# When the fifth and sixth unit make their sums: later quarter sums and sums of x, keys turned ahead of sums, one weight difference on VectorE

## The chip, the cores and the metric

The kernel runs on one core of one Trainium2 chip. The metric is the device time of one execution in microseconds; lower is better. The core's engines have queues of their own that run in order: TensorE (PE in the profile; its weight loads are PEld), VectorE (DVE), ScalarE (ACT), GpSimd (POOL) and SyncE (SP), which here mostly issues DMAs. They wait for each other on semaphores.

## The reference

Two layers, one after the other, all in float32. The first is a recurrence over 768 tokens for 4 batches and 8 heads of 48 dimensions. The second takes the 3072 x 384 result `x` through two weight matrices of 384 x 2048 and 2048 x 384.

```python
# first layer, for each batch and head; w is a decay per key dimension, u a bonus
for t in range(S):
    cur = einsum('d,e->de', u * k[t], v[t])
    y[t] = einsum('d,de->e', r[t], state + cur)
    state = w[t][:, None] * state + einsum('d,e->de', k[t], v[t])
# second layer
h = x @ w_in
g = h * (1.0 / (1.0 + np.exp(-h)))
out = g @ w_out
```

## The kernel before, in words

**Units.** The 768 tokens are cut into 6 blocks of 128, and the 4 batches into 2 pairs: 12 units, `i` = 0 to 11, each of one block for one pair. The text calls them unit 0 to unit 11, so the fifth and sixth unit are units 4 and 5.

**First layer.** Within a block the recurrence is done by levels: level `l` pairs neighbouring runs of 2^l tokens. Per unit, raw `w`, `k` and `r` are turned into `tw`, `tk`, `tr` (`turn`, line 361, transposes on VectorE); products of decays are made on GpSimd (`product`, 410); keys and queries are multiplied by them (`grow_keys`, 642, and `grow_own`, 651, on GpSimd; `grow_queries`, 624, and `prepare`, 779, on VectorE); TensorE multiplies queries and keys (`burst`, line 700); VectorE or ScalarE keep the right parts in the tile `score` (`keep_level`, 718 and 800). Products within groups of 8 tokens go another way: GpSimd multiplies (`block_bonus`, 493), VectorE sums (`block_sum` 0 to 4, line 530, into `block_sums`), DMAs move the sums through DRAM into `block_both` (`block_move`), and `block_turn` (563) and `block_write` (569) put the two halves of the heads into `score`. At the unit's end TensorE makes the output (`y_state` and `y_values`, 843 to 864) and the state's update (`update`, 909), and VectorE adds the update (932) after the old state was multiplied by the decays (914 on GpSimd up to unit 3, 927 on ScalarE later).

**Second layer.** For units 0 to 2 the first product is made plainly (`up`, line 1078, eight pieces, each followed by a Silu on ScalarE into a tile `gt`). From unit 3 on it is made by a fast scheme with 20 products (`first_part`, line 1185) of sums of weights and sums of x. The sums of weights are made once, by `in_weight_sum` (line 1124): `q7`, `q8` and so on, each a difference or sum of two 128x512 parts. The sums of x are made for each unit by `sums_of_x`, steps 0 to 7 (lines 1146 to 1166, VectorE). Between the 20 products VectorE joins partial results (`join`, line 1212) and ScalarE copies them (1206, 1209, 1228), in PSUM banks that the next products add to. The second product is made by seven quarter products (`quarter`, line 1329), three of which take sums of `gt` that `sums` makes on VectorE (line 1300): s1 is an addition; s2 = s1 - lower[0]; s3 is a difference; s4 = upper[0] - s2. In the list `made` of `sums` the places are 0: s1, 1: s3, 2: s2, 3: s4. The quarter products run in the order gt, gt, s2, s1, s3, s4, gt; results leave by ScalarE (1334) or by an addition on VectorE (1337, to `temps` or `ob`), and a later quarter product adds to the same bank, so it waits for that read. `sums(i, m)` makes the sums of piece m: two pieces of 128x512 from unit 3 on, four of 128x256 (m = 0 to 3) for units 1 and 2.

**Order.** No scheduler decides: each engine's queue is the order in which the Python code issues. For each `i` from 3 to 11 the loop at the end takes the seven quarter products of unit i-2 and the first products of unit i-1 as a list of steps, and the groups of unit i's first layer from `mix(i)`; each group has a count, and after the group's operations so many steps are issued:

```python
        for group, count in groups:
            do(*group)
            for step in steps[:count]:
                do(*step)
            steps = steps[count:]
```

So unit 4's stretch holds the second product of unit 2, the first product of unit 3 and the first layer of unit 4. Within it, VectorE's queue holds sums of gt, joins, sums of x and first-layer work, in the order of the groups. `NPAIR` is 4, `NFAST` 3, `FH` 8, and `j` is i-1. `in_weight_sum` operations are added to the groups of units 3 and 4 by place, with the engine beside the place.

Of the kernel before, what the change touches and what calls it, by code (L numbers as in the profile page):

```python
# [38 lines left out]
def kernel(  # L39
# [11 lines left out]
    nc = tc.nc  # L51
# [5 lines left out]
    NB = 2  # L57
# [11 lines left out]
    NPAIR = 4  # L69
# [389 lines left out]
    at = 768  # L459
# [495 lines left out]
    def both(fn, i, *args):  # L955
        return [(fn, i, b, *args) for b in range(NB)]
# [4 lines left out]
    def mix(i):  # L961
# [18 lines left out]
        def products_of(j, *ls):  # L980
            return [(product, j, l) for l in ls]

        end = [[*at(ahead, *bonus_steps(i + 1, 0, 1, 2, 3))],
               [*at(i < len(units) - NB, (turn_apart, i), (turn_k, i)), (y_state, i), *both(y_values, i), *at(ahead, *turns(i + 1)), *at(ahead and i > NFAST, *sum_steps(i + 1, 0, 1)),
                *at(i <= NFAST, (sums, i - 1, FH // 2 - 2)), *both(update, i), *at(not ahead, (move_x, i))]]
        if i < NPAIR:
            groups = [[*both(turn, i, "w"), (product, i, 0)],
                      [*both(turn, i, "k"), (odd_ones, i)], [*both(turn, i, "r"), (start_levels, i), (prepare_keys, i, 1)],
                      [(prepare, i, 1), *[(product, i, l) for l in range(1, NL)]],
                      [(burst, i, 1), (keep_level, i, 1)],  # L990
                      [(keep_level, i, 2), (go_on, i, 2)],
                      [(prepare, i, 3), (reverse_v, i), (bonus, i, 0), (bonus_sum, i, 0)],
                      [(bonus, i, 1), (burst, i, 3), (keep_level, i, 3), (bonus, i, 2)],
                      [(keep_level, i, 4), (go_on, i, 4), (bonus_sum, i, 1), (load_rk, i + 1), (load_u,)],
                      [(prepare, i, 5), (make_block_mask,), (bonus_spread, i)],
                      [(burst, i, 5), (keep_level, i, 5, 0), (keep_level, i, 6, 0), (go_on, i, 6), *at(i == NPAIR - 1, *both(turn, i + 1, "w")), (bonus_write, i, (0,)), (keep_level, i, 5, 1), (keep_level, i, 6, 1), (bonus_write, i, (1,))], *end]
            groups = list(zip(groups, (1, 1, 0, 2, 1, 1, 1, 1, 1, 2, 2, 1, 1)))
        else:
            j = i - 1
            if i <= NPAIR:  # L1000
                groups = [([*both(turn, i, "r"), (grow_own, i, 0), (x_out, j)], 2),
                          ([*start(i), *bonus_steps(i, 4), (x_in, j), (reverse_v, i)], 1),
                          ([(grow_queries, i, 2), (sums_of_x, j, 0)], 1),
                          ([(odd_keys, i, 2), (grow_keys, i, 2, False), (sums_of_x, j, 1)], 1),
                          ([(sums_of_x, j, 2), *sum_steps(i, 2), (prepare, i, 3), *bonus_steps(i, 5, 6, 7), (sums_of_x, j, 3, 4, 5, 6)], 2),
                          ([(burst, i, 3), (keep_level, i, 3)], 2),
                          ([*sum_steps(i, 3)], 1),
                          ([], 1),
                          ([*sum_steps(i, 4), (keep_level, i, 4)], 2),
                          ([(go_on, i, 4)], 1),  # L1010
                          ([], 1),
                          ([*at(ahead, (load_rk, i + 1, (0, 1), nc.scalar)), (block_move, i, False), (block_move, i, True), *at(ahead, (load_rk, i + 1, (2,)))], 1),
                          ([], 1),
                          ([(sums_of_x, j, 7)], 1),
                          ([(prepare, i, 5)], 2),
                          ([], 1),
                          ([(burst, i, 5), (keep_level, i, 5, 0), (keep_level, i, 6, 0), (go_on, i, 6), (block_turn, i), (block_write, i, 1)], 2),
                          ([(keep_level, i, 5, 1), (keep_level, i, 6, 1)], 1),
                          ([(block_write, i, 0), *at(i == NPAIR, *both(turn, i + 1, "w"))], 1),
                          ([*end[0], *at(i == NPAIR, *products_of(i + 1, 0))], 2), (end[1], 0)]  # L1020
            else:
                keys_2 = [(odd_keys, i, 2), (grow_keys, i, 2, False), (grow_queries, i, 2), *sum_steps(i, 2)]
                keys_3 = [(prepare, i, 3), *bonus_steps(i, 5)]

                def loads(name, *gs):
                    return [(load_blocks, i + 1, name, g) for g in gs if ahead]

                groups = [([*both(turn, i, "r"), *at(j == NPAIR, (sums, j - 1, 1, (1, 3))), (grow_own, i, 0), (x_out, j, nc.sync), *loads("w", 0, 1)], 2),
                          ([*at(j >= NPAIR, (add_update, j)), *start(i), *bonus_steps(i, 4), (x_in, j, nc.sync), *loads("w", 2, 3), (reverse_v, i)], 1),
                          ([*keys_2, *loads("k", 0, 1)], 1),  # L1030
                          ([*keys_3, *at(NPAIR + 1 < i < len(units) - 1, (sums_of_x, j, 0, 1)), *loads("k", 2)], 1),
                          ([*at(i in (NPAIR + 1, len(units) - 1), (sums_of_x, j, 0, 1)), (sums_of_x, j, 2), *bonus_steps(i, 6, 7), (sums_of_x, j, 3, 4, 5, 6), *loads("k", 3)], 2),
                          ([(burst, i, 3), *sum_steps(i, 3), (keep_level, i, 3), *sum_steps(i, 4)], 2),
                          ([(block_move, i, False), *at(ahead, (load_rk, i + 1, (0, 1))), *at(ahead and i > NPAIR + 1, (turn, i + 1, 0, "w"))], 1),
                          ([*loads("r", 0)], 1),
                          ([(block_move, i, True), *at(i == NPAIR + 1, (turn, i + 1, 0, "w")), *at(ahead, (turn, i + 1, 1, "w"), *products_of(i + 1, 0, 1, 2)), (keep_level, i, 4)], 2),
                          ([(go_on, i, 4), *at(ahead, *products_of(i + 1, 3, 4, 5, 6))], 1),
                          ([*at(ahead, (load_rk, i + 1, (2,)))], 1),
                          ([*loads("r", 1)], 1),
                          ([*at(ahead, (load_values, i + 1))], 1),  # L1040
                          ([(sums_of_x, j, 7)], 1),
                          ([(prepare, i, 5), *loads("r", 2)], 2),
                          ([*loads("r", 3)], 1),
                          ([(burst, i, 5), (keep_level, i, 5, 0), (keep_level, i, 6, 0), *at(ahead, *bonus_steps(i + 1, 0)), (go_on, i, 6), (block_turn, i), *at(i > NPAIR + 1, (block_write, i, 1))], 2),
                          ([(keep_level, i, 5, 1), (keep_level, i, 6, 1)], 1),
                          ([*at(i == NPAIR + 1, (block_write, i, 1)), (block_write, i, 0)], 1),
                          ([*at(ahead, *bonus_steps(i + 1, 1, 2, 3)), ], 2),
                          (end[1], 0)]

# [254 lines left out]
    def quarter(i, which):  # L1304
# [34 lines left out]
        if which >= 5 or final and which in (1, 4):  # L1339
# [96 lines left out]
    for i in range(3, len(units)):  # L1436
# [51 lines left out]
```

## Time and profile before

| | |
|---|---|
| median of 3 runs | 572.47 us (571.69 to 572.49) |
| the profiled execution | 571.82 us, span 570.0 us |
| granted TensorE clock | 0.997 |
| TensorE busy | 556.4 us, 98% |
| VectorE busy | 477.6 us, 84% |
| GpSimd busy | 396.8 us, 70% |
| ScalarE busy | 270.6 us, 47% |
| moved by DMA | 57.59 MB, 99 GB/s of HBM traffic over the span |

The span runs from the first to the last instruction. A timeline row gives start, length, engine, line, operation, output<-input, the shape, how many instructions were merged into the row, and in brackets the idle time of the engine before it and what ended that. A wait row gives who waited for whom, the total, the number of times and the longest. A windows row gives a stretch, its length, the busy time and instructions of PE, PEld, DVE, ACT and POOL, the granted clock, DMA share and GB/s. Line numbers are those of the kernel before; in the kernel after, lines from 983 to 1346 are one higher, and lines after `SOON` two or more.

### The profile page before, as it was taken

The page shows a single profiled execution, that of the slowest core. Times are in us where ns is not written, and L with a number is a line of the kernel's source. Part 1 is how long each engine was busy: PE and PEld are TensorE (multiplying, and loading weights), DVE is VectorE, ACT ScalarE, POOL GpSimd, SP SyncE. Part 2 cuts the span into 40 slices and gives each one's busy share as a digit, 9 for nine tenths or more (in the row PEclk, how much of TensorE's full clock was granted, in tenths as well). Part 3 has the DMA queues.
Part 4 walks back from the last instruction along what each step waited for, and adds up shares of the span by engine and source line. Part 5 has one row for each costly group of instructions (what it writes and reads, how often), then busy time and mean ns, then how long its engine had stood idle before and what let it go on. Part 6 is the DMA issues. An engine that isn't in the chain of part 4 may idle for free.

```text
span 570.0 us, 18875 instructions
## 1 busy us (share of the span) xinstructions
PE 556.4 (98%) x7782; PEld 517.9 (91%) x7782; DVE 477.6 (84%) x745; ACT 270.6 (47%) x604; POOL 396.8 (70%) x450
## 2 busy tenths in 40 slices
PE   8989999999998999899999999999999999999997
PEld 7768776698888999899999999999999999999997
DVE  7979798898999899879989989989989989882250
ACT  5779695442451373273274274274274272371330
POOL 6998868637999998795696696696696696700000
PEclk9989999999999999999999999999999999999999
DMA  9957776444255365265464465365465462102000
GB/s 224 316 114 204 183 230 113 49 84 101 74 90 100 69 112 94 58 130 93 73 129 89 87 120 94 71 128 94 93 106 96 91 109 65 37 6 56 29 9 21
DMA packets 206485, 57.59 MB, mean 101 GB/s; under 512 B 186048, under 2 KB 198208, under 8 KB 206400
## 3 DMA queue, kind: packets, MB, share of 16 engines
q1 hardware_dynamic: 203712, 54.23, 46.3%
q10 hardware_dynamic: 2688, 2.16, 1.6%
q8 instruction: 61, 1.00, 0.8%
q14 instruction: 24, 0.20, 0.1%
HBM read 47.14 MB, written 9.18 MB: 99 GB/s over the span
## 4 chain that ended last, share of the span: by engine, by line
PE 76%; DVE 9%; POOL 8%; issue 2%; DMA 2%; ACT 1%; SPq 1%; DVEq 0%; POOLq 0%
PE p_o L1329 24%; PE p_o L1185 15%; PE p_h L1185 10%; PE p_h L1078 6%; PE p_h L1329 4%; PE p_m L1267 4%; POOL tk L642 2%; PE p_sc L700 2%; PE p_m L864 2%; DVE temps L1300 2%; PE p_sc L1329 2%; DVE score L718 2%; PE p_m L843 1%; PE p_m L700 1%; DMA raw<-in_r_dram 1%
## 5 line engine op out<-in xcount | busy, mean ns | idle before, releaser
L642 POOL TENSOR_TENSOR tk<-tk,tw 128x256 f32<-128x256 f32 x112 | 93.2, 853 | 7.1 <-DVE tw L410 3.1
L1329 PE MATMUL p_o<-own,temps 128*128 128x192 f32 x496 | 82.9, 326 | 1.5 <-DVE temps L1300 1.5
L1329 PEld LDWEIGHTS p_o<-own,temps 128*128 128x128 f32 x496 | 80.8, 190 | 1.8 <-DVE temps L1300 1.8
L1185 PE MATMUL p_o<-xt,w_in_sb 128*64 128x128 f32 x1152 | 72.1, 273 | 0.6 <-POOL w_in_sb L1124 0.6
L1078 PE MATMUL p_h<-xt,w_in_sb 128*128 128x256 f32 x288 | 67.7, 391 | 0.8 <-POOL w_in_sb L260 0.8
L1185 PEld LDWEIGHTS p_o<-xt,w_in_sb 128*64 128x64 f32 x1152 | 64.7, 137 | 0.8 <-POOL w_in_sb L1124 0.8
L1078 PEld LDWEIGHTS p_h<-xt,w_in_sb 128*128 128x128 f32 x288 | 54.7, 194 | 9.4 <-POOL w_in_sb L260 1.1
L410 POOL TENSOR_TENSOR tw<-tw 128x256 f32<-128x256 f32 (+6 forms) x71 | 38.8, 546 | 33.0 <-DVE tw L361 29.6
L1329 PE MATMUL p_o<-w_out_sb,gt 128*128 128x192 f32 x308 | 54.4, 329 | 1.4 <-DVE ob L1337 1.4
L493 POOL TENSOR_TENSOR ruk<-tokens_rk 128x384 f32<-128x384 f32 x48 | 54.3, 1151 | 0.0
L1329 PEld LDWEIGHTS p_o<-w_out_sb,gt 128*128 128x128 f32 x308 | 50.1, 190 | 2.3 <-DVE ob L1337 1.7
L624 DVE TENSOR_TENSOR tr<-tr,tw 128x512 f32<-128x512 f32 x57 | 51.1, 896 | 0.6
L651 POOL TENSOR_TENSOR tk<-tk,tw 128x256 f32<-128x256 f32 x32 | 24.8, 806 | 30.7 <-DVE tk L361 30.7
L1300 DVE TENSOR_TENSOR temps<-gt 128x512 f32<-128x512 f32 (+1 forms) x48 | 44.6, 965 | 0.0
L1334 ACT COPY partial<-p_o 128x192 f32<-128x192 f32 x31 | 9.9, 319 | 70.5 <-PE p_o L1329 70.5
L612 ACT COPY tk<-tk 128x256 f32<-128x256 f32 x52 | 21.0, 403 | 38.0 <-POOL tk L642 29.0
L1209 ACT ACTIVATE gt<-p_o 128x512 f32<-128x512 f32 x45 | 26.1, 601 | 25.6 <-PE p_o L1185 25.6
L718 DVE COPY_PREDICATED score<-mask,p_sc 128x512 f32<-128x512 int8 x42 | 31.2, 798 | 0.8 <-PE p_sc L700 0.6
L1329 PE MATMUL p_o<-w_out_sb,temps 128*128 128x192 f32 x176 | 30.4, 326 | 0.0
L493 POOL TENSOR_TENSOR spare<-tokens_rk 128x384 f32<-128x384 f32 x24 | 29.1, 1228 | 0.6
L1329 PE MATMUL p_h<-w_out_sb,gt 128*128 128x192 f32 x168 | 29.1, 326 | 0.0
L1329 PEld LDWEIGHTS p_o<-w_out_sb,temps 128*128 128x128 f32 x176 | 28.9, 190 | 0.0
(252 smaller groups left out, 1308.0 us busy)
## 6 DMA issues: line engine op xcount, KB each, us to landing
w_out_sb<-in_moe_w_in_dram SPq DMA_DIRECT2D x6, 768.0 KB, 6.9
turned<-yt SPq DMA_DIRECT2D x18, 192.0 KB, 2.7
xt<-turned SPq DMA_DIRECT2D x9, 384.0 KB, 3.3
w_out_sb<-in_moe_w_out_dram SPq DMA_DIRECT2D x4, 768.0 KB, 5.1
own<-in_moe_w_out_dram SPq DMA_DIRECT2D x4, 768.0 KB, 6.5
tokens_w<-in_w_dram SPq DMA_DIRECT2D x8, 384.0 KB, 4.4
tokens_rk<-in_r_dram SPq DMA_DIRECT2D x7, 384.0 KB, 4.7
tokens_rk<-in_k_dram SPq DMA_DIRECT2D x7, 384.0 KB, 5.7
```

Of the source, the lines that this page charges most:

```text
L410: engine.tensor_tensor(out=up, in0=t[:, :, 0::2], in1=t[:, :, 1::2], op=ALU.mult)
L493: mul = lambda out, one, two: nc.gpsimd.tensor_tensor(out=out, in0=one, in1=two, op=ALU.mult)
L624: nc.vector.tensor_tensor(out=odd, in0=odd, in1=tw[i][l][:, :, 0::2][:, :, :, None].to_broadcast([128, Q, L >> (l + 1), c]), op=ALU.mult)
L642: nc.gpsimd.tensor_tensor(out=out, in0=have, in1=odd_products(i, l, b, *blocks), op=ALU.mult)
L651: nc.gpsimd.tensor_tensor(out=have, in0=have, in1=odd_products(i, l, b, [2, NP * ni]), op=ALU.mult)
L718: nc.vector.copy_predicated(out=dst, mask=masks[l][:, :, None].to_broadcast([128, NB, NP, ni, c]), data=sc[e].rearrange("p (b q) (i c) -> ...
L1078: nc.tensor.matmul(p_h[:, a, :], lhsT=w_in_sb[:, c, f * 128:(f + 1) * 128], rhs=xt[i][:, c, :], start=(a == 0 and c == 0), stop=(a == 1 an ...
L1185: nc.tensor.matmul(p[h:h + PD, q, :], lhsT=left[:, f:f + PD], rhs=right, start=first and q == 0, stop=q == 3, skip_group_check=True)
L1209: nc.scalar.activation(out=g(f, t), in_=have, func=AF.Silu)
L1267: nc.tensor.matmul(po[i, b], lhsT=gt[i, f // 2][:, f % 2, b * L:(b + 1) * L], rhs=w_out_sb[:, f, :], start=(f == 0), stop=(f == FC - 1))
L1300: nc.vector.tensor_tensor(out=out, in0=one, in1=two, op=op)
L1329: nc.tensor.matmul(p, lhsT=left(f), rhs=right[:, f, :], start=which in (0, 1, 3) and f == 0, stop=f == FH - 1, skip_group_check=True)
```

## The change

It moves operations of units 4 and 5 within their queues and gives one to another engine; no operation is added or removed, no DMA is moved, and the queues of TensorE, ScalarE and SyncE keep their order.

- Sums of pieces 2 and 3 of unit 2: s1 and s2 stay at the end of unit 3's stretch; s3 of both pieces goes into unit 4's group 0 behind the turning of r, and s4 of both into group 1.
- Sums of x of unit 3: steps 0 to 2 go together into group 4 of unit 4, steps 3 to 6 from group 4 behind the masked copies of group 5, and step 7 from behind the 10th first product to behind `prepare(4, 5)` and the 13th.
- s1 and s2 of piece 1 of unit 3 go behind the turning of unit 5's keys.
- Block sum 2 of unit 5 goes from group 2 to group 4, behind `prepare(5, 3)` (779) and the addition to `ob` (1337).
- The write of block half 1 of unit 5 goes from group 18 to group 16, as in the later units.
- The weight difference q7 goes from GpSimd, group 5, to VectorE, group 6, of unit 4.

```diff
         end = [[*at(ahead, *bonus_steps(i + 1, 0, 1, 2, 3))],
-               [..., *at(ahead, *turns(i + 1)), *at(ahead and i > NFAST, *sum_steps(i + 1, 0, 1)),
-                *at(i <= NFAST, (sums, i - 1, FH // 2 - 2)), *both(update, i), ...]]
+               [..., *at(ahead, *turns(i + 1)), *at(i == NPAIR, (sums, j, 1, (0, 2))), *at(ahead and i > NFAST, *sum_steps(i + 1, 0, 1)),
+                *at(i <= NFAST, (sums, i - 1, FH // 2 - 2, SOON[i == NFAST])), *both(update, i), ...]]
...
-                groups = [([*both(turn, i, "r"), (grow_own, i, 0), (x_out, j)], 2),
-                          ([*start(i), *bonus_steps(i, 4), (x_in, j), (reverse_v, i)], 1),
-                          ([(grow_queries, i, 2), (sums_of_x, j, 0)], 1),
-                          ([(odd_keys, i, 2), (grow_keys, i, 2, False), (sums_of_x, j, 1)], 1),
-                          ([(sums_of_x, j, 2), *sum_steps(i, 2), (prepare, i, 3), *bonus_steps(i, 5, 6, 7), (sums_of_x, j, 3, 4, 5, 6)], 2),
-                          ([(burst, i, 3), (keep_level, i, 3)], 2),
+                late = FH // 2 - 2, FH // 2 - 1
+                groups = [([*both(turn, i, "r"), *[(sums, j - 1, m, (1,)) for m in late], (grow_own, i, 0), (x_out, j)], 2),
+                          ([*start(i), *bonus_steps(i, 4), (x_in, j), *[(sums, j - 1, m, (3,)) for m in late], (reverse_v, i)], 1),
+                          ([(grow_queries, i, 2)], 1),
+                          ([(odd_keys, i, 2), (grow_keys, i, 2, False)], 1),
+                          ([(sums_of_x, j, 0, 1, 2), *sum_steps(i, 2), (prepare, i, 3), *bonus_steps(i, 5, 6, 7)], 2),
+                          ([(burst, i, 3), (keep_level, i, 3), (sums_of_x, j, 3, 4, 5, 6)], 2),
...
+                          ([], 1),
+                          ([(prepare, i, 5)], 2),
                           ([(sums_of_x, j, 7)], 1),
-                          ([(prepare, i, 5)], 2),
-                          ([], 1),
...
-                keys_2 = [(odd_keys, i, 2), (grow_keys, i, 2, False), (grow_queries, i, 2), *sum_steps(i, 2)]
+                keys_2 = [(odd_keys, i, 2), (grow_keys, i, 2, False), (grow_queries, i, 2), *at(i > NPAIR + 1, *sum_steps(i, 2))]
...
-                          ([*at(i in (NPAIR + 1, len(units) - 1), (sums_of_x, j, 0, 1)), (sums_of_x, j, 2), ...], 2),
+                          ([*at(i == NPAIR + 1, *sum_steps(i, 2)), *at(i in (NPAIR + 1, len(units) - 1), (sums_of_x, j, 0, 1)), (sums_of_x, j, 2), ...], 2),
...
-                          ([(burst, i, 5), ..., (block_turn, i), *at(i > NPAIR + 1, (block_write, i, 1))], 2),
+                          ([(burst, i, 5), ..., (block_turn, i), (block_write, i, 1)], 2),
                           ([(keep_level, i, 5, 1), (keep_level, i, 6, 1)], 1),
-                          ([*at(i == NPAIR + 1, (block_write, i, 1)), (block_write, i, 0)], 1),
+                          ([(block_write, i, 0)], 1),
...
+    SOON = range(4), (0, 2)
...
-            made[-1].append((sums, i, 1, range(4) if i > NFAST else (0, 2)))
+            if i > NFAST:
+                made[-1].append((sums, i, 1))
...
-        steps[-1].append((sums, i, FH // 2 - 1))
+        steps[-1].append((sums, i, FH // 2 - 1, SOON[i == NFAST - 1]))
...
-            for place, engine, names in ((5, nc.gpsimd, ("q7",)),
+            for place, engine, names in ((6, nc.vector, ("q7",)),
```

More of the change, by code (lines that the diff above doesn't have):

```diff
@@ L981, in products_of @@
             return [(product, j, l) for l in ls]
+        j = i - 1
         end = [[*at(ahead, *bonus_steps(i + 1, 0, 1, 2, 3))],
-               [*at(i < len(units) - NB, (turn_apart, i), (turn_k, i)), (y_state, i), *both(y_values, i), *at(ahead, *turns(i + 1)), *at(ahead and i > NFAST, *sum_steps(i + 1, 0, 1)),
-                *at(i <= NFAST, (sums, i - 1, FH // 2 - 2)), *both(update, i), *at(not ahead, (move_x, i))]]
+               [*at(i < len(units) - NB, (turn_apart, i), (turn_k, i)), (y_state, i), *both(y_values, i), *at(ahead, *turns(i + 1)), *at(i == NPAIR, (sums, j, 1, (0, 2))), *at(ahead and i > NFAST, *sum_steps(i + 1, 0, 1)),
+                *at(i <= NFAST, (sums, i - 1, FH // 2 - 2, SOON[i == NFAST])), *both(update, i), *at(not ahead, (move_x, i))]]
         if i < NPAIR:
@@ L998, in mix @@
         else:
-            j = i - 1
             if i <= NPAIR:
-                groups = [([*both(turn, i, "r"), (grow_own, i, 0), (x_out, j)], 2),
-                          ([*start(i), *bonus_steps(i, 4), (x_in, j), (reverse_v, i)], 1),
-                          ([(grow_queries, i, 2), (sums_of_x, j, 0)], 1),
-                          ([(odd_keys, i, 2), (grow_keys, i, 2, False), (sums_of_x, j, 1)], 1),
-                          ([(sums_of_x, j, 2), *sum_steps(i, 2), (prepare, i, 3), *bonus_steps(i, 5, 6, 7), (sums_of_x, j, 3, 4, 5, 6)], 2),
-                          ([(burst, i, 3), (keep_level, i, 3)], 2),
+                late = FH // 2 - 2, FH // 2 - 1
[5 more added lines that the diff above has]
+                          ([(burst, i, 3), (keep_level, i, 3), (sums_of_x, j, 3, 4, 5, 6)], 2),
                           ([*sum_steps(i, 3)], 1),
@@ L1031, in mix @@
                           ([*keys_3, *at(NPAIR + 1 < i < len(units) - 1, (sums_of_x, j, 0, 1)), *loads("k", 2)], 1),
-                          ([*at(i in (NPAIR + 1, len(units) - 1), (sums_of_x, j, 0, 1)), (sums_of_x, j, 2), *bonus_steps(i, 6, 7), (sums_of_x, j, 3, 4, 5, 6), *loads("k", 3)], 2),
+                          ([*at(i == NPAIR + 1, *sum_steps(i, 2)), *at(i in (NPAIR + 1, len(units) - 1), (sums_of_x, j, 0, 1)), (sums_of_x, j, 2), *bonus_steps(i, 6, 7), (sums_of_x, j, 3, 4, 5, 6), *loads("k", 3)], 2),
                           ([(burst, i, 3), *sum_steps(i, 3), (keep_level, i, 3), *sum_steps(i, 4)], 2),
@@ L1043, in mix @@
                           ([*loads("r", 3)], 1),
-                          ([(burst, i, 5), (keep_level, i, 5, 0), (keep_level, i, 6, 0), *at(ahead, *bonus_steps(i + 1, 0)), (go_on, i, 6), (block_turn, i), *at(i > NPAIR + 1, (block_write, i, 1))], 2),
+                          ([(burst, i, 5), (keep_level, i, 5, 0), (keep_level, i, 6, 0), *at(ahead, *bonus_steps(i + 1, 0)), (go_on, i, 6), (block_turn, i), (block_write, i, 1)], 2),
                           ([(keep_level, i, 5, 1), (keep_level, i, 6, 1)], 1),
-                          ([*at(i == NPAIR + 1, (block_write, i, 1)), (block_write, i, 0)], 1),
+                          ([(block_write, i, 0)], 1),
                           ([*at(ahead, *bonus_steps(i + 1, 1, 2, 3)), ], 2),
```

## The prediction

> **What bounds the kernel now.** I read the page's busy times first, then TensorE's waits between 140 and 270 us, then the timelines of TensorE, VectorE and GpSimd around each wait. "Unit 4" and "unit 5" are the fifth and sixth (`i` = 4 and 5): TensorE works on them from 167 to 214 and from 214 to 260 us.
>
> ```profile
> PE 556.4 (98%) x7782; PEld 517.9 (91%) x7782; DVE 477.6 (84%) x745; ACT 270.6 (47%) x604; POOL 396.8 (70%) x450
> 258.00:570.00 312.00, 309.00 (x4656) 302.90 (x4656) 249.37 (x394) 133.21 (x321) 184.47 (x210) 1.00 0.40 77
> ```
>
> TensorE (first row's PE; first busy figure of the second, a stretch from 258 us) sets the time. The waits view has no TensorE wait after 258 us, so what is won before it should last to the end. Between 167 and 258 us it has five, listed as total, count, longest:
>
> ```profile
> PE p_o L1329 <- DVE temps L1300: 1.5, 1, 1.5
> PE p_o L1329 <- DVE ob L1337: 1.4, 1, 1.4
> PE p_m L850 <- DMA raw<-in_r_dram: 0.9, 1, 0.9
> PE p_o L1185 <- POOL w_in_sb L1124: 0.6, 1, 0.6
> PE p_m L700 <- POOL tk L642: 0.2, 1, 0.2
> ```
>
> With the timeline's digits: 1.47 + 1.38 + 0.88 + 0.56 + 0.23 = 4.52 us, all that can be won on this path. Three of them on TensorE's timeline (start, length, bracket: idle before):
>
> ```profile
> 178.45 6.12 PE L1329 MATMUL p_o<-own,temps 128*128 128x192 f32 x36 [1.47 <-DVE temps L1300]
> 202.05 1.09 PE L1185 MATMUL p_o<-xt,w_in_sb 128*64 128x128 f32 x16 [0.56 <-POOL w_in_sb L1124]
> 231.77 2.87 PE L1329 MATMUL p_o<-w_out_sb,gt 128*128 128x192 f32 x16 [1.38 <-DVE ob L1337]
> ```
>
> The VectorE rows that end or explain the waits:
>
> ```profile
> 172.32 1.92 DVE L1300 TENSOR_TENSOR temps<-gt 128x256 f32<-128x256 f32 x2
> 174.16 0.72 DVE L1300 TENSOR_TENSOR temps<-temps,gt 128x256 f32<-128x256 f32 x1
> 174.92 0.95 DVE L1300 TENSOR_TENSOR temps<-gt,temps 128x256 f32<-128x256 f32 x1
> 175.79 1.12 DVE L932 TENSOR_TENSOR state<-p_sc,state 48x384 f32<-48x384 f32 x2
> 176.94 1.03 DVE L1300 TENSOR_TENSOR temps<-gt 128x256 f32<-128x256 f32 x2
> 177.89 0.51 DVE L1300 TENSOR_TENSOR temps<-temps,gt 128x256 f32<-128x256 f32 x1
> ...
> 187.95 0.71 DVE L779 TENSOR_TENSOR tr<-tr,tw 128x512 f32<-128x512 f32 x1
> ...
> 194.62 0.70 DVE L1212 TENSOR_TENSOR p_o<-gt,p_h 128x512 f32<-128x512 f32 x1 [1.21 <-PE p_h L1185]
> ...
> 229.56 1.13 DVE L530 TENSOR_REDUCE block_sums<-ruk 128x4 f32<-128x192 f32 x4 [0.89 <-POOL ruk L493]
> ...
> 254.30 3.61 DVE L569 COPY_PREDICATED score<-spare 128x1024 f32<-128x1024 int8 x2 [0.72 <-ACT score L800]
> ```
>
> And GpSimd:
>
> ```profile
> 200.66 1.34 POOL L1124 TENSOR_TENSOR w_in_sb<-w_in_sb,raw 128x512 f32<-128x512 f32 x1
> ...
> 220.34 1.65 POOL L651 TENSOR_TENSOR tk<-tk,tw 128x256 f32<-128x256 f32 x2 [1.97 <-DVE tk L361]
> ```
>
> VectorE has no idle time between 172.32 and 193.42, so in unit 4 an operation put later there does not vanish; it makes something else late.
>
> **Late sums of unit 2 (the 1.47 us wait).** Four rows are pairs s1, s3, then s2, s4, of pieces 2 and 3. TensorE stops at 176.98 for s2 of piece 3, which ends at 178.40. Without both s3 and both s4 ahead of it: s1 0.92 and s2 0.76 end at 174.00; the state addition (L932) needs GpSimd's multiplication, which ends at 174.60, so 0.6 idle; 1.15 for the addition, 0.48 and 0.54 for s1 and s2: 176.8. The wait goes. The moved s3 land at about 180.8 and are needed at 182.3, in the third quarter product; the s4 land at about 184.2 and are needed at 184.2 and 184.9, so little cover there. What is late next: up to L779 VectorE has the same work as before plus the 0.6 idle, so L779 ends at 189.2, not 188.6. The second half of the scores (TensorE L700, 190.21 before) would like to start at 188.74 and must wait until about 189.25. Gain left: 190.21 - 189.25 = 0.96 us. Bounds: nothing, if the moved sums run at their slow rows (up to 0.96 for 128x256 against 0.42 to 0.54); 1.47, if all run fast.
>
> **q7 on VectorE, later sums of x.** `sums_of_x` steps 0 to 2 stay ahead of L779, so nothing changes there; steps 3 to 6 (2.4 us) only swap with the masked copies, and their first reader is at 196.95. q7 is new on VectorE: the trace has this shape from L1124 there at 0.93 a piece (1.86 for two at 149.69), the nearest row; the bounds are 0.67 (fastest 128x512 addition) and 1.52 (slowest). It stands ahead of the join L1212, which had 1.21 us of idle. Before, VectorE was free at 193.42; now 193.42 + 0.6 + 0.93 = 194.95, the join ends 0.65 later at 195.6, and the product that needs it (196.08 before, 195.12 wanted) starts 0.5 late. Gain left 0.45. GpSimd loses one L1124 (1.25 from start to start); its next key row needs ScalarE's copy at about 196.75, so it runs 0.9 earlier and the weight waited for at 202.0 is there at 201.1. The product that waited 0.56 then starts at 201.1, not 202.05: gain 0.95 at the end of unit 4, where 1.47 + 0.56 = 2.03 are removed and 1.08 given back.
>
> The Trainium skill (Perfetto Trace Analysis, Optimizing Scalar/DVE Operations) speaks against such a move: since GpSimd and VectorE share a read port, shifting work between them might not help. By that rule the 0.56 would stay and the total below would be 2.8, not 3.3; the rows above (1.25 against 0.93) lean the other way, but no run yet shows q7 on VectorE.
>
> Step 7 of the sums of x (0.9 us) moves behind L779 into 0.70 us of VectorE idle (203.12 to 203.82); its readers, at 206.84 and later, are far off, but VectorE then leaves unit 4 only about 0.75 earlier.
>
> **Keys of unit 5 ahead of s1, s2 of unit 3.** The two transposes (219.56 before) move up by the 2.17 us of the two sums, so GpSimd's idle 1.97 goes and its chain in unit 5 runs some 2.3 to 2.9 earlier. The sums end at 220.78 - 0.75 = 220.0; TensorE wants them from 221.12 - 0.95 = 220.17. Cover 0.15; one slow row more (0.8) costs 0.65. I take 0.1: gain 0.85.
>
> **Block sum 2 of unit 5 behind L1337 (the 1.38 us wait).** It stalled VectorE 0.89 and ran 1.05 ahead of L779 and `ob`, for which TensorE waited. Now `ob` ends at 229.65 - 0.75 = 228.9, and TensorE wants it at 230.39 - 0.85 = 229.5. All 1.38 goes, with 0.6 to spare. GpSimd's last bonus step waits for block sum 2, but is due only at about 235.
>
> **Block write 1 of unit 5 (the 0.88 us wait).** The row blames a DMA, but TensorE starts at 257.97, just when the two masked writes end (257.91): I read it as those. Now the first goes ahead of the join at 252.89 (1.77 idle there), and only one, 2.0 us, is left for the end: ready near 253.4, wanted at 254.7. All 0.88 goes. It waits for small loads of `block_both`, the last landing at 250.75 before; their store follows a block sum that now comes some 2.3 earlier, so 248.5. If the load stayed at 250.75, the join would be 1.2 late. The 0.23 wait hangs on GpSimd's chain, which now leads by more than TensorE: gone. No DMA changes place on any queue.
>
> **Sum.** 0.85 + 1.38 + 0.88 + 0.23 = 3.34 us. The profiled execution took 571.82 (span 570.0 and 1.82 around it), so it becomes 568.5; the median shown, 572.47, is 0.65 higher, and becomes 569.1.
>
> **Rivals.**
> A. Unit 4 gives back everything: slow rows on a VectorE that is full. Unit 5 still brings 2.5: 570.0. For: the full queue. Against: the same operations in the same total.
> B. Nothing is given back, all 4.5 goes: 568.0. For: the joins and scores may be fed in time if the sums run fast.
> C. The turned keys wait. The chain of waits shows a load landing at 219.48, just ahead of their 219.56. Were it binding, VectorE would stand until 218.8, the sums would be ready at 222.2, 2.0 late: 3.34 - 1.9 = 1.4, 571.0. Against: the keys' own loads were issued by 186, and VectorE was never idle there.
> D. Slower: VectorE's two-input operations run slow in the new order, because GpSimd is never idle beside them. In unit 4 the seven that are fast now cost 0.5 to 0.7 more each, 4.1 us: L779 at 193.3, scores 3.1 later than before. In unit 5, eight 128x512 additions and products lead up to `ob`; 0.7 more each is 5.6, of which the trace already holds 1.2: `ob` 4.4 later, at 233.3, TensorE 1.6 later than before there, less 0.23 and 0.88: +0.5. Together +3.6: 576.1. It beats the gain once about half of these rows turn slow. Against: GpSimd was busy 17.4 of 18 us beside the fast rows already. The Trainium skill (SBUF — State Buffer, SBUF: two separate sides) gives such a mechanism: the pair of ports is locked for a whole instruction and the other engine blocks. The trace agrees in part only: L624 took 0.70 at 224.53 with GpSimd busy throughout.
> E. The waits have other owners than I read, as with the 0.88, and the time hardly moves: 572.
>
> **How the numbers follow.** Forecast 0.46, A 0.20, B 0.15, C 0.08, D 0.06, E 0.05. A measurement here can tell about 0.2%, 1.14 us, from no change. Faster: forecast, A, B and most of C, 0.86; within: E and the rest of C, 0.08; slower: D, 0.06. The range, 567.8 to 571.0, holds the forecast's own bounds, A, B and C's price.
>
> **What would show it.** Right: TensorE's waits on L1300, L1337, L850 and L1124 gone between 167 and 258 us, new short ones at the scores and behind the first join of unit 4, GpSimd's 1.97 idle gone. Wrong: a TensorE wait over 1 us in unit 4, VectorE idle ahead of the turned keys, or new TensorE waits after 255 us that give the gain back.

## The result, and the profile after

The changed kernel takes 574.99 us (median of 6, 573.39 to 575.58) against 572.45 for the kernel before in the same comparison: ratio 1.0044, 95% interval 1.0031 to 1.0057. It is slower by 2.5 us; 569.1 was forecast. The profiled execution has a span of 573.1 us (570.0 before) and a granted clock of 0.994 (0.997).

The page's busy times, same columns as before:

```profile
PE 558.9 (98%) x7782; PEld 519.4 (91%) x7782; DVE 486.7 (85%) x746; ACT 270.7 (47%) x604; POOL 398.6 (70%) x449
```

VectorE has one operation more, q7 (0.90 us), but is busy 9.1 us longer: the rest are the same operations, grown longer. TensorE's waits between 140 and 270 us:

```profile
PE p_o L1186 <- DVE temps L1338: 2.4, 1, 2.4
PE p_o L1186 <- DVE p_o L1213: 0.8, 2, 0.6
PE p_o L1330 <- DVE ob L1338: 0.7, 2, 0.4
PE p_o L1330 <- DVE temps L1301: 0.7, 2, 0.5
PE p_m L700 <- DVE tr L779: 0.6, 1, 0.6
```

Three of the five old waits (0.88, 0.56, 0.23) are gone, and the two largest have shrunk: 1.47 to 0.46 (L1301, its longest), 1.38 to 0.28 (`ob`). The first row is new and larger than any before. Its place on TensorE's timeline, in unit 5, at the second product behind the scores:

```profile
239.61 1.35 PE L1186 MATMUL p_o<-xt,w_in_sb 128*64 128x128 f32 x16 [2.40 <-DVE temps L1338]
240.74 1.93 PE L1186 MATMUL p_o<-gt,raw 128*64 128x128 f32 x16
242.45 1.67 PE L1186 MATMUL p_h<-xt,raw 128*64 128x128 f32 x16
```

This product writes the PSUM bank that the last quarter addition (L1338, to `temps`) has to read first. The products after it are slow as well: 1.93 and 1.67 us for 16 matmuls that take 1.04 elsewhere. The stretches show the cause (columns as before; the granted clock is the third number from the end):

```profile
239.00:240.00 1.00, 0.39 (x8) 0.39 (x9) 1.00 (x3) 0.00 (x0) 0.15 (x1) 1.00 0.00 0
240.00:241.00 1.00, 1.00 (x18) 1.00 (x16) 1.00 (x3) 0.00 (x0) 0.00 (x0) 0.66 0.54 194
241.00:242.00 1.00, 1.00 (x12) 1.00 (x10) 1.00 (x3) 0.59 (x1) 0.00 (x0) 0.50 0.52 187
```

The granted clock falls to 0.50; the next two stretches, not shown, have 0.50 and 0.64, and from 244 us on it is 1.00 again. The missing shares, 0.34 + 0.50 + 0.50 + 0.36, are 1.70 us of full clock: the price of this wait beyond its own 2.40.

VectorE around it:

```profile
224.05 1.00 DVE L1301 TENSOR_TENSOR temps<-gt 128x512 f32<-128x512 f32 x1
224.98 1.22 DVE L1301 TENSOR_TENSOR temps<-gt,temps 128x512 f32<-128x512 f32 x1
226.12 1.49 DVE L624 TENSOR_TENSOR tr<-tr,tw 128x512 f32<-128x512 f32 x1
...
231.82 0.36 DVE L1338 TENSOR_TENSOR ob<-p_o,partial 128x192 f32<-128x192 f32 x1
232.09 1.12 DVE L530 TENSOR_REDUCE block_sums<-ruk 128x4 f32<-128x192 f32 x4
233.13 0.66 DVE L1147 TENSOR_TENSOR xt<-xt 128x256 f32<-128x256 f32 x1
...
236.20 1.09 DVE L1158 TENSOR_TENSOR xt<-gt,xt 128x128 f32<-128x128 f32 x1
237.21 1.08 DVE L1161 TENSOR_TENSOR spare<-gt,xt 128x128 f32<-128x128 f32 x1
238.22 1.08 DVE L1164 TENSOR_TENSOR spare<-xt 128x128 f32<-128x128 f32 x1
239.22 0.34 DVE L1338 TENSOR_TENSOR temps<-p_o,partial 128x192 f32<-128x192 f32 x1
```

The same places before:

```profile
223.28 0.67 DVE L1300 TENSOR_TENSOR temps<-gt 128x512 f32<-128x512 f32 x1
223.88 0.72 DVE L1300 TENSOR_TENSOR temps<-gt,temps 128x512 f32<-128x512 f32 x1
224.53 0.70 DVE L624 TENSOR_TENSOR tr<-tr,tw 128x512 f32<-128x512 f32 x1
...
231.35 0.36 DVE L1337 TENSOR_TENSOR ob<-p_o,partial 128x192 f32<-128x192 f32 x1
231.63 0.48 DVE L1146 TENSOR_TENSOR xt<-xt 128x256 f32<-128x256 f32 x1
...
234.74 0.68 DVE L1160 TENSOR_TENSOR spare<-gt,xt 128x128 f32<-128x128 f32 x1
235.35 0.28 DVE L1163 TENSOR_TENSOR spare<-xt 128x128 f32<-128x128 f32 x1
235.55 0.34 DVE L1337 TENSOR_TENSOR temps<-p_o,partial 128x192 f32<-128x192 f32 x1
```

The first three rows took 0.67, 0.72 and 0.70 us before. `ob` ends at 232.18, not at the 228.9 forecast (231.71 before). Then block sum 2 and seven sums of x stand ahead of the last quarter addition, and the seven sums take 6.1 us from start to start (233.13 to 239.22) instead of 3.9 (231.63 to 235.55). The addition starts at 239.22, while TensorE was ready at 237.2. The timeline marks no idle time of VectorE from 174.6 to 242.4.

GpSimd beside these rows, first after, then before:

```profile
223.76 1.89 POOL L651 TENSOR_TENSOR tk<-tk,tw 128x256 f32<-128x256 f32 x2
225.61 2.86 POOL L493 TENSOR_TENSOR ruk<-tokens_rk 128x384 f32<-128x384 f32 x2
...
237.10 2.04 POOL L493 TENSOR_TENSOR ruk<-tokens_rk 128x384 f32<-128x384 f32 x2
```

```profile
223.49 0.57 POOL L410 TENSOR_TENSOR both_b<-tw 128x32 f32<-128x32 f32 x1
224.13 0.55 POOL L410 TENSOR_TENSOR diag<-both_b 128x16 f32<-128x16 f32 x1
```

Rows that lie side by side come out about equally long: 1.49 for L624 against 1.43 for each L493 (2.86 for two), 1.00 and 1.22 against 0.95 (1.89 for two; the 1.22 reaches into the first 1.43), 1.08 against 1.02 (2.04 for two); and before, 0.67 to 0.72 against 0.55 to 0.57. I read this as the two engines taking turns, so that each row holds the other's work as well as its own. Beside small products a VectorE sum stays near its own length (0.68 at 259.82 before, where GpSimd is idle) and the small product pays; beside large ones the sum pays. In these traces the VectorE operations whose length varies so all have two inputs in SBUF. The reduction L530, which has one input (0.91 to 0.95 for 128x768), and the joins L1213 (0.66 to 0.72) and additions L1338 (0.34 to 0.36), which have one of their two in PSUM, keep their times in all kernels between 165 and 265 us. The Trainium skill (SBUF — State Buffer, SBUF: two separate sides) says just this: an instruction of VectorE with two SBUF inputs and one of GpSimd that reads SBUF exclude each other for the whole instruction. These rows agree, and e5 below tests it.

Measured between the starts of the first quarter products, unit 4 takes 46.61 us instead of 44.85 (+1.76), unit 5 takes 47.27 instead of 46.09 (+1.18).

### The profile page after: what moved, and what is told of

Same layout as the page of the kernel before. It is cut to its first block, busy times and chain, and to the rows that moved or that the text cites. A ratio compares the mean times of both kernels' runs of the same rounds, so it can differ in the third digit from the quotient of the medians.

```text
span 573.1 us, 18875 instructions
## 1 busy us (share of the span) xinstructions
PE 558.9 (98%) x7782; PEld 519.4 (91%) x7782; DVE 486.7 (85%) x746; ACT 270.7 (47%) x604; POOL 398.6 (70%) x449
## 4 chain that ended last, share of the span: by engine, by line
PE 72%; DVE 10%; DMA 6%; SPq 6%; POOL 4%; issue 2%; ACT 0%; ACTq 0%; DVEq 0%; POOLq 0%
PE p_o L1330 22%; PE p_o L1186 15%; PE p_h L1186 10%; PE p_h L1079 6%; PE p_h L1330 4%; PE p_m L1268 4%; PE p_sc L700 2%; PE p_m L864 2%; SPq L127 2%; PE p_sc L1330 2%; DMA vq<-in_v_dram 2%; PE p_m L843 1%; DVE temps L1301 1%; POOL tk L642 1%; PE p_m L700 1%
## 5 line engine op out<-in xcount | busy, mean ns | idle before, releaser
L493 POOL TENSOR_TENSOR ruk<-tokens_rk 128x384 f32<-128x384 f32 x48 | 53.2, 1130 | 0.0
L624 DVE TENSOR_TENSOR tr<-tr,tw 128x512 f32<-128x512 f32 x57 | 52.4, 919 | 0.6
L1301 DVE TENSOR_TENSOR temps<-gt 128x512 f32<-128x512 f32 (+1 forms) x48 | 45.5, 983 | 0.0
L493 POOL TENSOR_TENSOR spare<-tokens_rk 128x384 f32<-128x384 f32 x24 | 28.3, 1191 | 0.6
```

Of the source, the lines that this page charges most:

```text
L493: mul = lambda out, one, two: nc.gpsimd.tensor_tensor(out=out, in0=one, in1=two, op=ALU.mult)
L624: nc.vector.tensor_tensor(out=odd, in0=odd, in1=tw[i][l][:, :, 0::2][:, :, :, None].to_broadcast([128, Q, L >> (l + 1), c]), op=ALU.mult)
L1301: nc.vector.tensor_tensor(out=out, in0=one, in1=two, op=op)
```

## The experiments

All times are ratios to the kernel before in the same comparison, with their 95% intervals. Line numbers are each kernel's own, and the diffs show parts of the changed lines. Theory 1: VectorE is full in unit 4, its operations run slow beside GpSimd, and the lateness is carried into unit 5. Its later form 1b: VectorE's two-input operations wait out GpSimd's. Rival 2: the loss is made in unit 5, by the late block sum; rival 2b: by the late block sum alone.

**e1, only unit 5's edits** (on the kernel before).

```diff
+ *at(i == NPAIR, (sums, i - 1, 1, (0, 2)))     # keys of unit 5 ahead of s1, s2
+ *at(i == NPAIR + 1, *sum_steps(i, 2))         # block sum 2 late
+ (block_turn, i), (block_write, i, 1)          # block write 1 early
```

> The kernel before with the changes of unit 5's work alone: keys of unit 5 turned ahead of s1, s2 of unit 3, block sum 2 of unit 5 late, block write 1 of unit 5 early; sums of unit 2, sums of x of unit 3 and q7 stay as before. Theory 1 (VectorE is full in unit 4 and the reordered operations run slow beside GpSimd; the lateness is carried into unit 5): unit 4 is as before, so VectorE comes into unit 5 on time, the 1.4 us wait for ob and the 0.9 us wait at L850 go, the wait of the first product after the scores for the last quarter addition is under 1.5 us and leaves the clock at 1.00; 570.0 to 571.9 us, ratio to before 0.995 to 0.999. Rival 2 (the loss is made in unit 5 itself: block sum 2 ahead of the sums of x makes the last quarter addition late): that wait is 2 us or more with a lowered clock after it, as in the changed kernel, and the time is 573 to 575 us. Rival 3 (the five waits were not the price I read): 572.4 us.

Measured: 572.80 us, 1.0023 [1.0012, 1.0034], between the two ranges expected. With unit 4 as before, the large wait is there all the same:

```profile
239.04 1.09 PE L1185 MATMUL p_o<-xt,w_in_sb 128*64 128x128 f32 x16 [2.40 <-DVE temps L1337]
```

The clock falls behind it as in the changed kernel, and `ob` comes at 231.24, hardly earlier than before's 231.35. So the loss is made in unit 5, not carried in from unit 4: rival 2 stands, theory 1's carried lateness falls.

**e2, only unit 4's edits** (the changed kernel with unit 5's three edits undone).

> The kernel before with the changes of unit 4's work alone: late s3, s4 of unit 2, later sums of x of unit 3, q7 on VectorE. Theory 1: TensorE leaves unit 4 about 1.5 us later than before, as in the changed kernel (quarter products of unit 3 start near 216.1, not 214.5); unit 5 then has its old waits, partly taken up by the lateness: 573 to 575 us, ratio 1.001 to 1.004. Rival 2: unit 4 gains or is even, 571.5 to 572.4 us. My prediction's step for unit 4 would make it 571.5.

Measured: 572.23 us, 1.0007 [0.9998, 1.0016], no difference. Unit 5 starts 1.8 us later than before (216.28), yet the next unit starts at 260.77 (260.61 before): unit 5's old 1.38 us wait for `ob` is gone, because TensorE comes later. The wait of 0.89 us at L850 is labelled here with the masked write (L569), as the prediction read it.

**e3, block sum 2 back in its old place** (all else changed).

```diff
-  *at(i > NPAIR + 1, *sum_steps(i, 2))]
+  *sum_steps(i, 2)]
```

> The changed kernel with block sum 2 of unit 5 back in its old place, ahead of the query products L779 and of ob. Rival 2 expects the 2.4 us wait of the second product after the scores to go, and with it the lowered clock (1.7 us more): 571 to 572 us. Theory 1: block sum 2 runs ahead of ob instead of behind it, so TensorE waits about 1 us more for ob and about 1 us less behind the scores; VectorE's total is the same, and only the clock may stay up: 573.3 to 575 us.

Measured: 571.93 us, 1.0002 [0.9993, 1.0010]. The 2.4 us wait and the lowered clock are gone, and a 0.90 us wait for `ob` is back. In the changed kernel, moving this one reduction costs 1.0044 - 1.0002 = 0.0042, or 2.4 us (3.6 between the two profiled executions), where the prediction had it win 1.38.

**e4, the last quarter addition ahead of sums of x 3 to 6** (the changed kernel).

```diff
-  (sums_of_x, j, 2), *bonus_steps(i, 6, 7), (sums_of_x, j, 3, 4, 5, 6), ...
+  (sums_of_x, j, 2), *bonus_steps(i, 6, 7), ...
-  ([(burst, i, 3), *sum_steps(i, 3), ...
+  ([*at(i == NPAIR + 1, (sums_of_x, j, 3, 4, 5, 6)), (burst, i, 3), *sum_steps(i, 3), ...
```

> The changed kernel, but in unit 5 steps 3 to 6 of the sums of x stand behind the last quarter addition (L1338 to temps) instead of ahead of it: four operations of about 1 us each swap with one of 0.3 us. If the 2.4 us wait and the clock after it are the price as the trace shows them (theory 1 and rival 2 alike), the wait and the lowered clock go, 4.1 us, of which 1 to 2 us come back at the first join (VectorE's queue is no shorter): 572 to 573 us, ratio to the changed kernel 0.995. If the label of that wait is wrong, or the lowered clock has another cause: 574 to 575 us as the changed kernel.

Measured: 573.19 us, 1.0022 [1.0013, 1.0031], a little above the range. The addition comes at 236.00, wait and lowered clock are gone (2.40 + 1.70 = 4.1 us), but the sums are now late for the next reader, the first join:

```profile
243.73 1.09 PE L1186 MATMUL p_o<-gt,in_sum 128*64 128x128 f32 x16 [1.33 <-DVE p_o L1213]
```

Unit 5 gets 2.17 us shorter (45.10), so 1.9 of the 4.1 came back. The queue is too long whatever is put last in it.

**e5, without GpSimd's block products 5, 6 and 7 of unit 5** (the changed kernel; that part of the bonus is left out of the result).

> The changed kernel with GpSimd's block products 5, 6 and 7 (L493) of unit 5 left out: 12 GpSimd instructions, some 7 us between 232 and 239 us, are missing, so the products within groups of 8 tokens of that unit are not right. Theory 1b (VectorE's operations with two SBUF inputs wait for GpSimd's, one at a time): beside an idle GpSimd the seven sums of x from step 0 to 6 take 0.3 to 0.5 us each, 2.5 to 3.5 together instead of 6.1; the 2.4 us wait and the lowered clock go, and some of the joins' wait too: 570 to 571.5 us. Rival (the slow rows have another cause: their place, the transfers, the readers of x): they stay near 1 us each and so does the time, 574 to 575.

Measured: 570.63 us, 0.9978 [0.9968, 0.9988]. GpSimd has no row from 232.5 to 242.2, and VectorE's last sum of x and the addition read

```profile
235.22 0.28 DVE L1164 TENSOR_TENSOR spare<-xt 128x128 f32<-128x128 f32 x1
235.42 0.35 DVE L1338 TENSOR_TENSOR temps<-p_o,partial 128x192 f32<-128x192 f32 x1
```

The seven sums take 2.1 us instead of 6.1, in the same order with the same inputs: 0.42 each for 128x256, 0.28 or 0.29 for 128x128. The rows ahead of them, where GpSimd still works, keep the lengths of the changed kernel (1.00, 1.22, 1.49). This shows the contention and gives its size: up to 0.8 us for each small sum.

**e6, only the early block write** (on the kernel before).

> The kernel before with block write 1 of unit 5 moved ahead alone. Both theories: nothing ahead of it changes, so the 0.9 us wait at L850 goes and the other four stay: ratio to before 0.9985, about 0.9 us less. If the wait was the load's after all, or the masked write ahead of the join makes the last product late: 1.000 or above.

Measured: 571.20 us, 0.9991 [0.9976, 1.0007]. The wait at L850 is gone, the other four stay (1.6, 1.4, 0.6 and 0.2 us). The interval includes no change and is wide: two of the twelve executions took 574.7 and 574.9 us. One of them is the profiled one, and there unit 4 starts nearly 4 us late (173.51 against 169.67), ahead of everything that was edited.

**e7, the changed kernel without the keys ahead.**

> The changed kernel with unit 5's keys turned behind s1, s2 of unit 3 again. Theory 1b: turning the keys ahead filled GpSimd's idle 2 us and put its products beside VectorE's sums; with it undone the sums from s1 to L779 run 1 to 2 us shorter in all, the wait behind the scores is under 1.5 us and the clock stays up: 571.5 to 573 us. Rival 2b (the late block sum 2 alone makes the last quarter addition late, whatever the keys do): wait 2 us or more with the lowered clock, 574 to 575 us.

Measured: 571.26 us, 0.9989 [0.9980, 0.9997], a little better than theory 1b had it. GpSimd's chain of unit 5 starts at 220.20 again, its small products stand beside s3, s4 and the first L624, and these take 0.68, 0.72 and 0.70 us; the sums of x fall beside key products (3.25 us for four) and 128x192 products (1.85 for three) and take 0.56 to 0.82, the last one 0.28. `ob` comes at 229.97, the last quarter addition at 235.55. So the late block sum alone does not make the long wait; rival 2b falls. Both edits are needed for it: the keys put GpSimd's long products beside VectorE's sums, the block sum puts the last quarter addition behind those.

**e8, keys ahead and early block write** (on the kernel before, block sum in its old place).

> The kernel before with the keys of unit 5 turned ahead and block write 1 early, block sum 2 in its old place. By my prediction's steps GpSimd comes 2 us earlier, block sum 2 no longer stalls VectorE (0.89 us), and the waits of 0.9 and 0.2 us go: 2.0 us less, ratio 0.9965. Theory 1b: the 0.89 us are taken back by slow rows from s1 to L779 (1.9 us in the run with unit 5's part alone), so TensorE's wait for ob stays or grows to 2.4 us; with the 0.9 us of the write and the 0.2 of the keys the ratio is 0.999 to 1.001.

Measured: 570.97 us, 0.9978 [0.9970, 0.9987]: faster than the kernel before by an interval that excludes 1, and between what the prediction's steps (0.9965) and theory 1b (0.999 and above) gave. TensorE's waits between 140 and 270 us:

```profile
PE p_o L1329 <- DVE ob L1337: 1.8, 1, 1.8
PE p_o L1329 <- DVE temps L1300: 1.6, 1, 1.6
PE p_o L1185 <- POOL w_in_sb L1124: 0.6, 1, 0.6
```

The rows L1300 to L624 are as slow as in the changed kernel (1.00, 1.22, 1.49), so the wait for `ob` grows to 1.8; but the waits of 0.88 and 0.23 are gone, and the clock stays at 1.000. The brackets understate what goes with such a wait: from the start of L843 to the next unit TensorE now takes 3.46 us instead of 4.65, 1.19 less for the 0.88.

The last four kernels start from the kernel before with the late block sum and the early block write, and add unit 4's edits one by one.

**e9, nothing added.**

> The kernel before with block sum 2 of unit 5 late and block write 1 early; keys, sums and q7 stay as before. Theory 1b (only the keys ahead of the sums bring GpSimd's products beside VectorE's sums): the sums of x keep their 3.9 us, the last quarter addition ends near 235.7, the waits of 1.38 and 0.88 us go, those of 1.47, 0.56 and 0.23 stay, and the time falls by 1.5 to 2.2 us, a ratio of 0.9962 to 0.9974. Rival (VectorE is full ahead of the sums of x in any order): since unit 4 gives up nothing here, the sums of x with the block sum ahead of them again delay the last quarter addition, and a wait of 1 us or more appears behind the first product after the scores: ratio 0.999 to 1.001.

Measured: 571.09 us, 0.9989 [0.9976, 1.0002], between what theory and rival gave. As 1b said, the last quarter addition comes at 235.42 and no wait exceeds 1 us there; but with the 1.38 and 0.88 us waits gone, two new ones stand behind: 0.58 for that addition and 0.64 for the first join. Unit 5 is 1.07 us shorter (45.02), about half of the 2.26 removed.

With e6, e8 and e1 this makes a table of four kernels that have the early write and unit 4 as before, and differ only in the two edits: neither 0.9991 (e6, with the wide interval), keys ahead 0.9978 (e8), late block sum 0.9989 (e9), both 1.0023 (e1). The interval of e1 lies above those of the other three. Neither edit costs anything alone; together they lose 0.0032 to 0.0045, or 1.8 to 2.6 us.

**e10, with the late s3 and s4 of unit 2.**

```diff
+ [*both(turn, i, "r"), *[(sums, j - 1, m, (1,)) for m in (2, 3)], (grow_own, i, 0), ...]
+ [*start(i), ..., (x_in, j), *[(sums, j - 1, m, (3,)) for m in (2, 3)], (reverse_v, i)]
```

> As the one with the late block sum and the early write, and s3 and s4 of pieces 2 and 3 of unit 2 moved as in the change; sums of x of unit 3 and q7 as before. If the moved sums are what costs unit 4 its time: the 1.47 us wait falls to about 0.5, a wait of 0.4 to 0.6 us comes at the scores, and unit 5 begins no earlier than before (214.4 to 214.7) but not 1.6 us later either, since q7 is still on GpSimd; ratio like the kernel without them, within 0.001. If the moved sums alone gave unit 4's whole loss, unit 5 would begin near 216 and the ratio would be 0.002 higher.

Measured: 573.63 us, 1.0037 [1.0023, 1.0051]. Only one line of the expectation holds: the 1.47 us wait falls to 0.46. Two larger ones come, for `ob` and for the last quarter addition of unit 4:

```profile
188.99 2.87 PE L1329 MATMUL p_o<-w_out_sb,gt 128*128 128x192 f32 x16 [1.89 <-DVE ob L1337]
196.10 1.09 PE L1185 MATMUL p_o<-xt,w_in_sb 128*64 128x128 f32 x16 [2.13 <-DVE temps L1337]
```

It is unit 5's failure over again, in unit 4: the sums of x 3 to 6 stand ahead of the addition, beside GpSimd's 128x384 products and a weight difference, and take 1.09, 1.09, 1.08 and 1.34 us. Unit 4 takes 49.09 us instead of 44.85.

**e11, with q7 on VectorE.**

> As the one with the late block sum and the early write, and q7 on VectorE; no sum of unit 2 or of x is moved. The sums of x 3 to 6 of unit 3 stay ahead of the masked copies. If q7 on VectorE is what costs: the join after it comes about 0.9 us later, a wait of 0.4 to 0.7 us at the product behind it, the 0.56 us wait for the weight gone, so the start of unit 5 is within 0.3 us of before; the ratio within 0.0006 of the kernel without it. If it runs beside GpSimd at twice its length, the start of unit 5 is 1 us later and the ratio 0.0015 higher.

Measured: 571.08 us, 0.9981 [0.9972, 0.9989], like e7 and e8 faster than the kernel before by an interval that excludes 1. q7 took 1.09 us, the wait for the weight is gone, and no wait stands behind the first join of unit 4, where 0.4 to 0.7 us was expected. Unit 4 still takes 44.89 us (44.85 before). Up to the last first products it runs 0.47 us ahead of before (38.44 us into the unit against 38.91); these then lose 0.5 us, where the trace names no releaser beyond "issue". e10, without q7, has such a gap (0.29) at the same place, so the cause of this loss stays open.

**e12, with the late sums of unit 2 and q7 on VectorE.**

> As the one with the late block sum and the early write, with the late sums of unit 2 and q7 on VectorE; sums of x of unit 3 as before. Against the changed kernel this leaves out the keys ahead and the move of the sums of x in unit 4. Theory 1b: the sums of x of unit 5 keep 3.9 us, and the ratio is 0.9965 to 0.9985. If the losses of the late sums and of q7 add up to unit 4's 1.6 us, unit 5 begins near 216; if the moved sums of x made that loss, near 214.5 to 215.

Measured: 573.82 us, 1.0037 [1.0025, 1.0049]; waits of 1.89 and 2.12 us as in e10. The expected 0.9965 to 0.9985 looked at unit 5 alone, and unit 5 begins at 218.89, later than either place expected. Against e7 (0.9989), which differs from it only by the moved sums of x, it shows what that move is for: with it unit 4 loses 1.7 us, without it 4.

## Why the prediction was wrong, point by point

- **The bound and the five waits** were read rightly: TensorE's path sets the time, and the owners are as read (the 0.88 is the masked writes: e6 removes it by moving the write alone, e2 names it).
- **Block sum 2 behind L1337: "All 1.38 goes, with 0.6 to spare."** This is the step that failed, together with the next. It asked only when `ob` would be ready. Block sum 2 left one queue place and took another, ahead of the last quarter addition, on which the second product behind the scores waits. The prediction did not look at that addition. The wait for `ob` did fall, to 0.28. Even without the keys ahead, this place gives back 0.58 and the join 0.64 (e9); with them it costs 2.40 and, in the profiled execution, 1.70 of lowered clock. Undoing this edit alone brings 1.0044 to 1.0002 (e3).
- **Keys ahead: "cover 0.15 ... I take 0.1".** GpSimd's idle 1.97 did not vanish (2.04 after), but its chain in unit 5 begins 1.4 us earlier (218.94 against 220.34) while VectorE's s3 of unit 3's piece 1 begins 0.8 later (224.05 against 223.28), so the two lines slid by some 2 us against each other. s3, s4 and L624 were left at before's rows, 0.67 to 0.72; they took 1.00, 1.22 and 1.49. A row's length belongs to the pair of instructions that meet, and the edit changes who meets whom. `ob` ended 3.3 us later than the forecast 228.9: about half of it is slow rows (8.13 us from s3 to the end of `ob`, against 8.43 before less 1.94 for block sum 2 and its stall), the other half is VectorE coming to s3 0.8 late instead of 0.75 early. Undoing this edit alone brings 1.0044 to 0.9989 (e7).
- **Unit 4: gain 0.95 (0.85 in the sum).** Measured between the starts of the first quarter products, a loss of 1.76, below the bounds given. The 1.47 us wait went to 0.46 and the 0.56 went, much as forecast, but new waits came for `ob` (0.43), at the scores (0.61) and behind the first join (0.61). The step "up to L779 VectorE has the same work as before plus the 0.6 idle" gave L779's end at 189.2; it ended at 190.95, the moved sums and the first L624 running at slow rows (0.94 and 0.83 for each moved sum, 1.48). q7 was priced well: 0.93 forecast, 0.90 and 1.09 measured. But the gain that its move was to bring did not last to the end of unit 4: with it alone the 0.56 us wait goes and unit 4 is no shorter (e11: 44.89). The rule of the Trainium skill that was weighed there (Perfetto Trace Analysis, Optimizing Scalar/DVE Operations), that such a move might not help, fits the length of unit 4 in e11; but the 0.56 that was to stay by it went, and what took its place is open. With unit 4's edits alone the loss did not show in the total, because unit 5 had waits to take it up (e2).
- **Block write and the 0.23:** right, 0.88 and 0.23 gone.
- **Rivals.** D, with a chance of 0.06, had the mechanism and nearly the size (+3.6 forecast, +2.5 measured). It was set low because L624 took 0.70 at 224.53 "with GpSimd busy throughout". GpSimd was busy there with the 128x32 to 128x8 products, of which one alone takes 0.20 to 0.24 (e8), and it was they that waited. Busy time said nothing; the size of the neighbour's instruction did. D's place was wrong: it put 3.1 us of the loss into unit 4 and ended unit 5 at `ob`'s own wait, but unit 5 was lost at the addition behind it. That its size came near is in part luck. Unit 4 gave back its gain, as A had it, and more; B, C and E did not happen.
- **The signs of being wrong.** None of those named came: the largest wait in unit 4 is 0.61, VectorE is not idle ahead of the turned keys, and no wait stands after 255 us. The loss came at a place that no sign covered.

## What to carry to other kernels

When an edit slides one of two contending engines against the other, price the moved operations by the instructions that will stand beside them, not by their rows of before: here the same 128x128 sum took 0.28 us alone and 1.08 beside 128x384 products. When an operation is put later in a queue, list every reader behind its new place; the reader that it was moved out of the way of is only the first. And price edits one by one on the chip, then in pairs: two edits that each cost nothing alone (e8, e9) lost 1.8 to 2.6 us together (e1).

## What the hardware showed that was not expected

**The length of a wait alone did not decide whether TensorE's clock fell.** In the changed kernel and in e1 the granted clock fell to 0.50 some 0.7 and 1.2 us after TensorE had resumed from the 2.40 us wait; by the stretches the loss is 1.70 us of full clock in each (e1: 0.39 + 0.50 + 0.50 + 0.31), that is 3.4 us at half clock. Waits of 1.81 us (e8) and 2.13 us (e10) left it at 1.00 in the profiled executions. But a shorter wait was followed by the same drop: before's trace shows 0.65, 0.50, 0.50 and 0.64 in the four stretches from 39 us on, 1.71 us missing, behind a wait of 1.53 us that ended at 37.76. The same wait, 1.53 to 1.58 us, is followed by the drop in the traces of before, the changed kernel and e1, and by none in those of e2, e3, e8 and e11. So a threshold can't be read from these runs.

What a drop costs depends on its place. The early one costs nothing that the runs show: in e1's comparison the executions of the kernel before with a mean clock of 0.997 have a median of 571.69 us, those with 1.000 have 572.15. The late one does cost: of the changed kernel's six executions, five have a mean clock of 0.994 and took 574.90 to 575.58 us, and one has 1.000 and took 573.39. So of the 2.5 us lost, some 1.6 hang on a drop that did not come in every execution. e1's eleven executions lie in two groups, six from 572.2 to 572.8 us and five from 574.0 to 574.8, the profiled one among the latter; the distance of their medians is 1.65 us, too. That the lower group kept its clock at that place is not shown, since most executions of both groups have a mean of 0.997.

The Trainium skill (TensorE: Matmul & The Clock Gate, Part 1: The HAM clock gate) has half clock after an idle window of about 3.4 us, counted in windows that run freely. The depth and the length agree, and windows that run freely would fit that the same wait has both outcomes; but waits of 2.40 and 1.53 us, shorter than such a window, were followed by the drop.

**GpSimd pays as well.** The products of 128x32, 128x16 and 128x8 took 0.57, 0.55 and 0.53 us beside VectorE's sums before, and 0.24, 0.22 and 0.20 in e8, where VectorE made transposes at that time. In before's trace they start 0.64 and 0.63 us apart, near the pace of VectorE's sums beside them (0.60 and 0.65).
